# A scheduling model inside the kernel: longer landings for the turned blocks, longer hand-overs between engines, new due times

## The chip, the cores and the metric

The kernel runs on one core of a Trainium2 chip. The metric is the device time of one execution in microseconds (us). Before the change the median of three runs was 1069.37 us (1068.89 to 1074.59).

## The reference

A linear attention with random features, followed by a two-layer network over all tokens:

```python
def phi(x):                       # q and k: (8, 8, 576, 64), scaled
    proj = np.einsum('bhsd,md->bhsm', x, omega)      # 128 features
    h = proj - np.sum(x * x, axis=-1, keepdims=True) / 2.0
    return np.exp(h - np.max(h, axis=-1, keepdims=True)) / np.sqrt(m)
kv = np.einsum('bhsm,bhsd->bhmd', phi(k), v)
z = np.sum(phi(k), axis=2)
attn = np.einsum('bhsm,bhmd->bhsd', phi(q), kv) / (np.einsum('bhsm,bhm->bhs', phi(q), z)[..., None] + 1e-06)
x = attn as (4608 tokens, 512)
h = x @ w_in                      # (512, 2048), float64 weights
out = np.where(h > 0.0, h, np.exp(np.minimum(h, 0.0)) - 1.0) @ w_out
```

## The kernel before

**The network.** 4608 tokens are cut into 12 blocks of 384, and 2048 hidden features into 16 steps f of 128. One step of a block is layer one (tile `ph`, lines 912 to 914: for each of four chunks c three matmuls on 384 columns, high and low halves of operands), the activation (ACT lines 921 and 922, DVE line 925, then `g` in a high and a low half), and layer two (`acc`, lines 950 to 952: for each of three groups of 128 tokens three matmuls on 512 columns). The first three blocks run in two halves of eight steps, while the weights are still being turned from float64 into pairs of float32 (`from_f64`, tile `u_w`; the second layer's halves `w2h`, `w2l` stay on the chip, the first layer's go to DRAM as `w1s` and come back step by step as `w1c`, three buffers). Steps are numbered through all blocks: ph_84, g_85, w1c_89 are steps 84, 85 and 89 of 192.

**The attention.** 64 heads make 32 pairs. Pair i goes through: load of xk, xq and v; projection and exponent for k (`ppk`, line 524, then `hk`); the same for q (`ppq`, `hq`); the state (`pkv`, line 616); the sum of k's features (`zs` on POOL, split into `zr` by ACT and DVE); `pz`, line 673, which spreads that sum; the denominators (`den`, DVE line 694); the normalised `hq` (POOL); then hq is turned so that features lie on partitions (`qh`), and `pn` (line 773) multiplies it with the state. pn goes into `xh` and `xl`, the input of layer one. Four pairs make a batch, 576 tokens, which later blocks of the network read; so attention of later tokens runs between the network's steps of earlier ones.

**The turned pairs.** For pairs 8 to 31 (`TURNED = 8`) hq is turned in three stages: DVE transposes 32 x 32 blocks (`tb`, line 739); one DMA writes them to DRAM (`turned`, line 746, 576 KB); four DMAs fetch them back in the other order (`qh`, line 751, 144 KB each). There is one buffer for qh and four in DRAM.

**What sets the order.** The kernel is written as a list of tasks. `Plan.op` takes a task's engine, its estimated duration, a due time, what it reads and writes, and the bytes of a DMA. `Plan.order` then plays the program through on a model of the chip: at each moment an engine that is free takes, among the tasks whose inputs are ready and whose buffers are free, the one with the earliest due time. The instructions are issued in the order in which the model started them, engine by engine, and each engine then runs its list strictly in that order. When a result counts as ready for the next engine is set by `LAT` (ns, from engine to engine), and a DMA's by `DMA_LAT` (twice, before and after the transfer) and `DMA_RATE`. Some tasks may go to either of two engines (`alt`); the model decides that too. All DMAs are issued by SP, one queue in order. The due times come from numbers at the head of the file: `MLP0`, `SEG`, `STEP`, `STEP_ATT` place the network's steps, `DUE_...`, `LOAD2`, `K2`, `KV2`, `Q2` say how long before its end a pair's parts are due, `EARLIER` brings the loads, projections, pz and denominators of turned pairs forward, and `CONV1` to `CONV3` place the weight conversions.

Of the kernel before, what the change touches and what calls it, by code (L numbers as in the profile page):

```python
# [18 lines left out]
P = 128  # L19
# [12 lines left out]
NJ = 9  # L32
# [8 lines left out]
NNAT = dict(k=7, q=8)  # L41


MLP0 = 44.09
SEG = [8.6, 6.25, 3.85, 5.29, 3.12, 5.81]
STEP = 5.38
STEP_ATT = 6.27

LAG = 3.3


PAIR0 = 9.09
DUE_LOAD, DUE_K, DUE_KV, DUE_Q = 23.0, 24.78, 13.79, 18.96
LOAD2, K2, KV2, Q2 = 69.42, 37.24, 24.66, 31.63
TAIL = 12.51
TAIL2 = 4.95


CONV1 = 12.88
CONV_STEP = -0.22  # L60
CONV2 = 0.04

EARLY = 23.2
CONV3 = 62.36


SPLIT = (0, 8, 16)
NHALF = 3

DUE_Z = 13.27  # L70


TURNED = 8
EARLIER = 6.61
QB = 32
NQB = P // QB
NTURN = 4


NONES = 8  # L80
# [27 lines left out]
class Plan:  # L108
# [2 lines left out]


    LAT = {
        "PE": dict(PE=0, ACT=230, DVE=196, POOL=200, SP=200),
        "ACT": dict(PE=270, ACT=200, DVE=145, POOL=207, SP=200),
        "DVE": dict(PE=250, ACT=128, DVE=127, POOL=203, SP=200),
        "POOL": dict(PE=150, ACT=150, DVE=150, POOL=102, SP=200),
        "SP": dict(PE=100, ACT=100, DVE=100, POOL=100, SP=100),
    }
    LOOSE = ("pa", "h")  # L120

    SHARED = ("DVE", "POOL")

    FREE = dict(PE=1300.0, ACT=1950.0, DVE=2100.0, POOL=1300.0, SP=700.0)
    DMA_LAT, DMA_RATE = 1100.0, 360.0

    def __init__(self):
        self.tasks, self.writer, self.readers = [], {}, {}

    def op(self, eng, ns, due, fn, reads=(), writes=(), nbytes=0, alt=None, port=False, after=0.0):  # L130
        n = len(self.tasks)
        engs = {eng: (ns, 0.0)}
        for e, *t in alt or ():
            engs[e] = tuple(t)
        f = fn if alt is not None else lambda e: fn()
        deps, bufs = set(), set()
        for k in reads:
            if k in self.writer:
                deps.add(self.writer[k])
            self.readers.setdefault(k, []).append(n)  # L140
        for k in writes:
            if k in self.writer:
                deps.add(self.writer[k])
            deps.update(self.readers.pop(k, ()))
            self.writer[k] = n
        for k in (*reads, *writes):
            b = k[0] if isinstance(k, tuple) else k
            if isinstance(b, Buf):
                bufs.add(b)
        deps.discard(n)  # L150
        for b in bufs:
            b.left += 1
        self.tasks.append((engs, due, f, deps, bufs, nbytes, port, after))

    def order(self):
# [7 lines left out]
        end = [0.0] * len(tasks)  # L163
        free, queue, events = {}, {}, [0.0]
        held = dict.fromkeys(self.SHARED, 0.0)
        slots, dma = {}, 0.0
# [47 lines left out]
        while len(done) < len(tasks):  # L214
            started = False
            for eng, q in queue.items():
                if free[eng] > now:
                    continue
                best, first = None, 0.0
                for n in q:  # L220
                    engs, due, _, _, bufs, _, port, _ = tasks[n]
                    if ready[n][eng] > now or (best is not None and due >= first):
                        continue
                    if eng == "DVE" and port and held["POOL"] > now or eng == "POOL" and held["DVE"] > now:
                        continue
                    if len(engs) > 1 and not mine(n, eng):
                        continue
                    for b in bufs:
                        if b.slot is None:
                            s = sum(z <= now for z in slots[b.key])  # L230
                            if s < (1 if line[b.key][-1] is b else 2 if b.key in self.LOOSE else 99):
                                break
                    else:
                        best, first = n, due
                if best is None:
                    continue
                started = True
                engs, _, _, _, bufs, nbytes, port, _ = tasks[best]
                for e in engs:
                    queue[e].remove(best)  # L240
                ns = engs[eng][0]
                for b in bufs:
                    if b.slot is None:
                        s = slots[b.key]
                        b.slot = s.pop(s.index(min(s)))
                        line[b.key].remove(b)
                free[eng] = now + ns
                if eng == "POOL" or eng == "DVE" and port:
                    held[eng] = now + ns
                if nbytes:  # L250
                    dma = max(now + self.DMA_LAT, dma) + nbytes / self.DMA_RATE
                    end[best] = dma + self.DMA_LAT
                else:
                    end[best] = now + ns
                heapq.heappush(events, free[eng])
                done.append((best, eng))
                for b in bufs:
                    b.left -= 1
                    if not b.left:
                        heapq.heappush(events, end[best] + 200.0)  # L260
                        slots[b.key].append(end[best] + 200.0)
                for u in users[best]:
                    for e in ready[u]:
                        ready[u][e] = max(ready[u][e], end[best] + self.LAT[eng][e])
                    waits[u] -= 1
                    if not waits[u]:
                        for e in ready[u]:
                            queue[e].append(u)
                            heapq.heappush(events, ready[u][e])
            if not started:  # L270
                if not events:
                    raise RuntimeError("no task can start")
                now = max(now, heapq.heappop(events))
# [33 lines left out]
def performer_elu_kernel(  # L307
# [14 lines left out]
    nc = tc.nc  # L322
# [35 lines left out]
    op = pl.op  # L358
# [297 lines left out]
    def finish(i, due):  # L656
# [24 lines left out]
        qh = Buf(sb, [P, 2, S], F32, "qh", f"qh_{i}", 1)  # L681
        for g in range(3):
            d = due - 9 + g - early
            js = slice(4 * g, min(4 * g + 4, NJ))
            n = js.stop - js.start
# [38 lines left out]
            def dst(x, g=g):  # L724
# [8 lines left out]
                alt=other("turn", "DVE", dve(n * P)),  # L733
            )
        if i >= TURNED:
            tb = Buf(sb, [P, NQB * NJ * QB], F32, "raw", f"tb_{i}", 4)

            def blocks():
                nc.vector.transpose(
                    out=tb().rearrange("p (n j c) -> p j n c", n=NQB, j=NJ),  # L740
                    in_=h().rearrange("p j (n c) -> p j n c", c=QB),
                )

            op("DVE", 1378, due - 10, blocks, [(h, "n", g) for g in range(3)], (tb,))
            qt = turned[i % NTURN]
            op("SP", 700, due - 9, lambda: nc.sync.dma_start(qt, tb()), (tb,), (("qt", i % NTURN),), P * P * NJ * 4)
            for m in range(NQB):

                def fetch(m=m):
                    r = slice(m * QB, (m + 1) * QB)  # L750
                    nc.sync.dma_start(
                        qh()[r].rearrange("p a (n x) -> p (a n) x", n=2),
                        qt[:, m * NJ * QB:(m + 1) * NJ * QB].rearrange("(n r) x -> r n x", r=QB),
                    )

                op("SP", 600, due - 8 + 0.1 * m, fetch, (("qt", i % NTURN),), ((qh, m),), QB * P * NJ * 4)

        kvf = kvs[i % 2]
        halves = [(slice(o, o + n), n, bank(i, "pa", f"pn_{i}_{o}")) for o, n in ((0, 256), (256, S - 256))]
# [50 lines left out]
    def from_f64(src, hi, lo, nm, due, key):  # L810
# [19 lines left out]
        def ui():  # L830
# [4 lines left out]
            "SP", 500, due - 10, lambda: nc.sync.dma_start(raw(), src), (), ((raw, 0), (raw, 1)), P * 4096,  # L835
            after=due - EARLY,
        )
# [35 lines left out]
    def weights(F, due):  # L873
# [8 lines left out]
        if blk == 0:  # L882
            from_f64(w1[f], lambda: t()[:, 0], lambda: t()[:, 1], f"w1_{f}", due, (t,))
            op("SP", 500, due, lambda: nc.sync.dma_start(w1s[f], flat()), both, (("w1s", f),), P * 4096)
            from_f64(w2[f], lambda: w2h[:, f], lambda: w2l[:, f], f"w2_{f}", due + CONV1 - (CONV2 if f < SPLIT[1] else CONV3), ("w2", f))
        else:
# [89 lines left out]

    begin, t = [], MLP0
    for n, (blk, f0, f1) in enumerate(SEGMENTS):
        begin.append(t)
        t += (f1 - f0) * (SEG[n] if n < len(SEG) else STEP if blk % 3 == 1 or blk >= NBLK - 2 else STEP_ATT)  # L980
    begin.append(t)
# [4 lines left out]
    def batch(b, n):  # L986

        t0, t1 = begin[n - 1], begin[n] - (TAIL if b < 2 else TAIL2)
        for hp in range(NHP):
            pair(b * NHP + hp, t0 + (t1 - t0) * (hp + 1) / NHP)  # L990

    def segment(n):
        blk, f0, f1 = SEGMENTS[n]
        F0 = sum(b - a for _, a, b in SEGMENTS[:n])
        for F in range(F0, F0 + f1 - f0):
            if blk:
                weights(F, step[F])
            layer1(F, step[F])
            layer2(F, step[F] + LAG * STEP)

    def convert(n):
        F0 = sum(b - a for _, a, b in SEGMENTS[:n])
        for e in range(SEGMENTS[n][2] - SEGMENTS[n][1]):
            weights(F0 + e, step[F0 + e] - CONV1 - CONV_STEP * e)

    warm()
    omega(MLP0 - TAIL + PAIR0 * (1 - NHP) - DUE_LOAD)
    for hp in range(NHP):
        pair(hp, MLP0 - TAIL + PAIR0 * (hp + 1 - NHP))
    convert(0)  # L1010
# [91 lines left out]
```

## Time and profile before

| what | before |
|---|---|
| median of three runs | 1069.37 us |
| profiled execution, its own time | 1065.02 us |
| its span | 1063.2 us |
| mean granted TensorE clock | 0.988 |
| moved by DMA | 205.24 MB, mean 193 GB/s |
| L912, L913, L914 (layer one), 768 each | 263.6, 258.6 and 259.1 us busy |
| L950, L951, L952 (layer two), 576 each | 231.3, 228.0 and 228.0 us busy |
| turned<-tb, 24 DMAs, median to landing | 3.2 us |
| qh<-turned, 96 DMAs, to landing, min, median, max | 2.3, 4.3 and 7.8 us |

The profile names engines PE (TensorE), DVE (VectorE), ACT (ScalarE), POOL (GpSimd) and SP. A row of a group gives the line, the engine, the operation, the tiles out<-in without their numbers, the shape, the count; then busy time and mean duration in ns; then how long the engine stood idle just before these instructions, and for what. A row of waits gives engine, tile and line, `<-` what released it, and the total in us, how many times, and the longest. A row of the timeline gives start and duration in us, and in brackets the idle time before it. Matmuls are pipelined: one starts before the last has ended, so the distance of two starts is what a matmul costs.

### The profile page before, as it was taken

The numbers are of one execution on the slowest core, as the hardware profiler recorded it, in microseconds if no ns is written. First come the engines' busy times: TensorE is split into PE (matmuls) and PEld (weight loads), VectorE is DVE, ScalarE is ACT, GpSimd is POOL, SyncE is SP. The second block draws the span as 40 slices with busy tenths as digits, with TensorE's granted clock in tenths as the row PEclk, the third lists the DMA queues.
The fourth block names the chain that finished last, engine by engine and source line by source line (L and its number), as shares of the span: only waits on it lengthen the run. The fifth ranks groups of instructions, "written<-read, shape, count | busy, mean of one in ns | idle before, by whom it ended". The sixth has DMA issues, their size and how long they took to land.

```text
span 1063.2 us, 19120 instructions
## 1 busy us (share of the span) xinstructions
PE 1023.1 (96%) x5923; PEld 899.9 (85%) x5923; DVE 651.1 (61%) x2453; ACT 697.4 (66%) x1887; POOL 414.2 (39%) x419
## 2 busy tenths in 40 slices
PE   8989899999999999999999899999989999999998
PEld 7878788988878788998778788889878888899987
DVE  7989978768877763236757775225777766322221
ACT  7988675569978773358877795327888886332322
POOL 3635433324544443234444454223444444222221
PEclk9989899999999999999999999999999999999999
DMA  8556486567786665435766656534657664443431
GB/s 219 187 186 220 174 280 215 214 228 263 243 294 213 193 209 180 165 114 206 230 202 220 215 201 229 166 132 162 213 181 234 201 204 142 161 159 131 149 131 58
DMA packets 70518, 205.24 MB, mean 193 GB/s; under 512 B 7952, under 2 KB 20432, under 8 KB 70416
## 3 DMA queue, kind: packets, MB, share of 16 engines
q1 hardware_dynamic: 70416, 204.01, 57.8%
q8 instruction: 48, 0.79, 0.3%
q14 instruction: 54, 0.44, 0.1%
HBM read 169.64 MB, written 34.34 MB: 192 GB/s over the span
## 4 chain that ended last, share of the span: by engine, by line
PE 70%; DVE 10%; DMA 8%; ACT 7%; issue 2%; SPq 1%; POOL 0%; DVEq 0%; ACTq 0%; POOLq 0%
PE ph L912 10%; PE acc L950 10%; PE ph L914 10%; PE ph L913 10%; PE acc L951 9%; PE acc L952 9%; DMA qh<-turned 5%; PE pn L773 2%; PE ppq L524 2%; PE ppk L524 2%; PE pkv L575 1%; PE pkv L616 1%; ACT hk L444 1%; DMA xq<-in_qx_dram 1%; ACT hq L444 1%
## 5 line engine op out<-in xcount | busy, mean ns | idle before, releaser
L367 POOL TENSOR_TENSOR g<-e,g 128x384 fp32r<-128x384 f32 x168 | 183.6, 1093 | 419.8 <-DVE g L364 335.4
L912 PE MATMUL ph<-xh,w1c 128*128 128x384 f32 x768 | 263.6, 343 | 0.1
L914 PE MATMUL ph<-xh,w1c 128*128 128x384 f32 x768 | 259.1, 337 | 0.0
L913 PE MATMUL ph<-xl,w1c 128*128 128x384 f32 x768 | 258.6, 337 | 0.0
L921 ACT ACTIVATE e<-ph 128x384 f32<-128x384 f32 x192 | 94.9, 495 | 233.0 <-PE ph L914 230.9
L925 DVE SCALAR_TENSOR_TENSOR e<-e,ph 128x384 f32<-128x384 f32 x192 | 105.7, 551 | 211.3 <-ACT e L922 210.4
L950 PE MATMUL acc<-w2h,g 128*128 128x512 f32 x576 | 231.3, 402 | 0.0
L951 PE MATMUL acc<-w2l,g 128*128 128x512 f32 x576 | 228.0, 396 | 1.6 <-DVE w2l L367 1.6
L952 PE MATMUL acc<-w2h,g 128*128 128x512 f32 x576 | 228.0, 396 | 0.0
L912 PEld LDWEIGHTS ph<-xh,w1c 128*128 128x128 f32 x768 | 145.0, 189 | 15.0 <-issue 2.5
L913 PEld LDWEIGHTS ph<-xl,w1c 128*128 128x128 f32 x768 | 144.9, 189 | 9.7
L914 PEld LDWEIGHTS ph<-xh,w1c 128*128 128x128 f32 x768 | 144.5, 188 | 0.0
L952 PEld LDWEIGHTS acc<-w2h,g 128*128 128x128 f32 x576 | 108.3, 188 | 25.5
L367 POOL TENSOR_TENSOR hq<-hq,den 128x512 f32<-128x512 f32 (+1 forms) x96 | 81.7, 871 | 101.9 <-DVE den L703 77.1
L950 PEld LDWEIGHTS acc<-w2h,g 128*128 128x128 f32 x576 | 108.5, 188 | 13.9 <-issue 2.9
L951 PEld LDWEIGHTS acc<-w2l,g 128*128 128x128 f32 x576 | 108.4, 188 | 11.4 <-DVE w2l L367 1.9
L922 ACT ACTIVATE e<-e 128x384 f32<-128x384 f32 x192 | 101.9, 532 | 3.3
L694 DVE CUSTOM_DVE_ANT_0 junk<-hq,pz 128x128 f32<-128x128 f32 (+1 forms) x320 | 73.6, 278 | 18.9 <-PE pz L673 17.4
L533 ACT ACTIVATE p2k<-ppk,sqk 128x128 f32<-128x128 f32 x225 | 69.9, 370 | 16.2 <-PE ppk L524 13.4
L860 POOL TENSOR_TENSOR u_w<-u_w,raw_w 128x512 int32<-128x512 int32 x32 | 46.6, 1458 | 76.2 <-DVE u_w L857 52.0
L542 DVE CUSTOM_DVE_ANT_0 hq<-ppq,p2q 128x128 f32<-128x128 f32 x216 | 53.2, 286 | 33.4 <-ACT p2q L533 32.2
L444 ACT ACTIVATE hk<-hk,mnk 128x128 f32<-128x128 f32 x225 | 72.0, 408 | 0.1
(101 smaller groups left out, 1539.5 us busy)
## 6 DMA issues: line engine op xcount, KB each, us to landing
w1c<-w1s SPq DMA_DIRECT2D x176, 512.0 KB, 3.3
raw_w<-in_w_dram SPq DMA_DIRECT2D x32, 512.0 KB, 4.5
xk<-in_kx_dram SPq DMA_DIRECT2D x25, 576.0 KB, 4.3
xq<-in_qx_dram SPq DMA_DIRECT2D x24, 576.0 KB, 5.6
turned<-tb SPq DMA_DIRECT2D x24, 576.0 KB, 3.2
qh<-turned SPq DMA_DIRECT2D x96, 144.0 KB, 4.3
v<-in_v_dram SPq DMA_DIRECT2D x32, 325.0 KB, 4.8
out_dram<-o SPq DMA_DIRECT2D x36, 256.0 KB, 3.4
```

The lines of the kernel that those rows point to most:

```text
L367: (nc.vector if e == "DVE" else nc.gpsimd).tensor_tensor(*args)
L444: nc.scalar.activation(h()[:, j, :], src(j), AF.Exp, bias=mn()[:, j:j + 1], scale=-1.0)
L694: nc.vector.tensor_tensor_reduce(out=junk()[r], in0=h()[r, j, :], in1=pz()[r, a * P:(a + 1) * P], scale=1.0, scalar=EPS, op0=ALU.mult, op1 ...
L912: nc.tensor.matmul(ph(), wh, xh[:, c, o:o + TB], start=(c == 0), stop=False)
L913: nc.tensor.matmul(ph(), wh, xl[:, c, o:o + TB], start=False, stop=False)
L914: nc.tensor.matmul(ph(), wl, xh[:, c, o:o + TB], start=False, stop=(c == NC - 1))
L921: op("ACT", act(TB, True), due, lambda: nc.scalar.activation(e(), ph(), AF.Relu, scale=-1.0), (p,), (e,))
L922: op("ACT", act(TB), due + 0.2, lambda: nc.scalar.activation(e(), e(), AF.Exp, scale=-1.0), (e,), (e,))
L925: lambda: nc.vector.scalar_tensor_tensor(e(), e(), -1.0, ph(), ALU.add, ALU.max), (p, e), (e,),
L950: nc.tensor.matmul(a(), g()[:, 0, ts], w2h[:, f], start=(f == f0), stop=False)
L951: nc.tensor.matmul(a(), g()[:, 0, ts], w2l[:, f], start=False, stop=False)
L952: nc.tensor.matmul(a(), g()[:, 1, ts], w2h[:, f], start=False, stop=(f == f1 - 1))
```

## The change

The model gets a new delay, `LAND`: the DMA that stores a turned tile and the four that fetch it count as landing 2000 ns later than by the formula. All entries of `LAT` between different engines grow, by 64 to 300 ns; `DMA_LAT` goes from 1100 to 1500 ns. A turned store or fetch thus counts 2.8 us more than before from issue to use. All due times are set anew; `EARLIER` grows by 4.39 us. No instruction of the program is changed, only the order in which the engines get them, and for tasks with `alt`, which engine. The core of the diff:

```diff
-MLP0 = 44.09
-SEG = [8.6, 6.25, 3.85, 5.29, 3.12, 5.81]
+MLP0 = 45.16
+SEG = [8.6, 5.97, 3.67, 5.16, 3.34, 5.69]
...
-LOAD2, K2, KV2, Q2 = 69.42, 37.24, 24.66, 31.63
+LOAD2, K2, KV2, Q2 = 72.76, 36.27, 29.03, 29.75
...
-CONV1 = 12.88
-CONV_STEP = -0.22
-CONV2 = 0.04
+CONV1 = 11.46
+CONV_STEP = 0.11
+CONV2 = 0.74
...
-CONV3 = 62.36
+CONV3 = 52.47
...
-EARLIER = 6.61
+EARLIER = 11.0
...
+LAND = 2000.0
...
-        "PE": dict(PE=0, ACT=230, DVE=196, POOL=200, SP=200),
-        "ACT": dict(PE=270, ACT=200, DVE=145, POOL=207, SP=200),
-        "DVE": dict(PE=250, ACT=128, DVE=127, POOL=203, SP=200),
-        "POOL": dict(PE=150, ACT=150, DVE=150, POOL=102, SP=200),
-        "SP": dict(PE=100, ACT=100, DVE=100, POOL=100, SP=100),
+        "PE": dict(PE=0, ACT=300, DVE=260, POOL=270, SP=300),
+        "ACT": dict(PE=500, ACT=200, DVE=215, POOL=280, SP=300),
+        "DVE": dict(PE=480, ACT=200, DVE=127, POOL=270, SP=300),
+        "POOL": dict(PE=400, ACT=230, DVE=230, POOL=102, SP=300),
+        "SP": dict(PE=400, ACT=200, DVE=200, POOL=200, SP=200),
...
-    DMA_LAT, DMA_RATE = 1100.0, 360.0
+    DMA_LAT, DMA_RATE = 1500.0, 360.0
...
-                    end[best] = dma + self.DMA_LAT
+                    end[best] = dma + self.DMA_LAT + self.lands[best]
...
-            op("SP", 700, due - 9, lambda: nc.sync.dma_start(qt, tb()), (tb,), (("qt", i % NTURN),), P * P * NJ * 4)
+            op("SP", 700, due - 9, lambda: nc.sync.dma_start(qt, tb()), (tb,), (("qt", i % NTURN),), P * P * NJ * 4, lands=LAND)
...
-                op("SP", 600, due - 8 + 0.1 * m, fetch, (("qt", i % NTURN),), ((qh, m),), QB * P * NJ * 4)
+                op("SP", 600, due - 8 + 0.1 * m, fetch, (("qt", i % NTURN),), ((qh, m),), QB * P * NJ * 4, lands=LAND)
```

What it moves is shown at three places, all of pair 17. In the rows a tile's first number is its pair or step, the last one only tells buffers apart; lines from 113 on are two higher in the changed file.

TensorE around pz_17, before: it stands behind the last part of layer one of step 84 and just ahead of layer two of step 82.

```order
L914 MATMUL ph_84_6123<-xh_88,w1c_84_5924 128x384
L524 MATMUL ppk_18_0_6148<-om_74,tk_18_5939 128x256 x2
L673 MATMUL pz_17_6157<-zr_17_6103,ones_72 128x256 x2
L524 MATMUL ppk_18_1_6160<-om_74,tk_18_5939 128x256 x2
L950 MATMUL acc_5_0_0_6013<-w2h_80,g_82_6088 128x512
```

TensorE around pz_17 in the changed order: it stands behind step 83's layer one, ahead of step 81's layer two and of all projections of pair 18.

```order
L916 MATMUL ph_83_6032<-xh_88,w1c_83_5855 128x384
L627 MATMUL pkv_17_6055<-ident_67,zs_17_5969 128x128
L675 MATMUL pz_17_6101<-zr_17_6071,ones_72 128x256 x2
L952 MATMUL acc_5_0_0_6042<-w2h_80,g_81_6006 128x512
L953 MATMUL acc_5_0_0_6042<-w2l_81,g_81_6006 128x512
```

So pz_17 has moved ahead by about one step of the network.

TensorE ahead of pn_17, before: layer two of step 85 and the first part of step 88's layer one.

```order
L912 MATMUL ph_88_6423<-xh_88,w1c_88_6255 128x384
L913 MATMUL ph_88_6423<-xl_89,w1c_88_6255 128x384
L914 MATMUL ph_88_6423<-xh_88,w1c_88_6255 128x384
L950 MATMUL acc_5_0_2_6050<-w2h_80,g_85_6302 128x512
L951 MATMUL acc_5_0_2_6050<-w2l_81,g_85_6302 128x512
L952 MATMUL acc_5_0_2_6050<-w2h_80,g_85_6302 128x512
L773 MATMUL pn_17_0_6436<-qh_17_6369,kvf1_77 64x256 x2
```

TensorE ahead of pn_17 in the changed order: the same, and one more part of step 88.

```order
L954 MATMUL acc_5_0_2_6074<-w2h_80,g_85_6340 128x512
L914 MATMUL ph_88_6447<-xh_88,w1c_88_6267 128x384
L915 MATMUL ph_88_6447<-xl_89,w1c_88_6267 128x384
L916 MATMUL ph_88_6447<-xh_88,w1c_88_6267 128x384
L775 MATMUL pn_17_0_6475<-qh_17_6326,kvf1_77 64x256 x2
```

So pn_17 has kept its place but for three matmuls, and the stretch between pz_17 and pn_17 has grown from its front.

SP around the store and the fetch of pair 17, before (`turned1` is the DRAM buffer; `xq_20` the load of a later pair's q):

```order
L887 DMA w1c_88_6255<-w1s_82 128x1024
L746 DMA turned1_85<-tb_17_6294 128x1152
L887 DMA w1c_89_6333<-w1s_82 128x1024
L417 DMA xq_20_6351<-in_qx_dram 128x1152
L751 DMA qh_17_6369<-turned1_85 32x4x288 x4
L887 DMA w1c_90_6401<-w1s_82 128x1024
```

SP at the same place in the changed order:

```order
L889 DMA w1c_87_6198<-w1s_82 128x1024
L748 DMA turned1_85<-tb_17_6206 128x1152
L889 DMA w1c_88_6267<-w1s_82 128x1024
L753 DMA qh_17_6326<-turned1_85 32x4x288 x4
L889 DMA w1c_89_6368<-w1s_82 128x1024
L419 DMA v_20_6379<-in_v_dram 128x650
L419 DMA xq_20_6390<-in_qx_dram 128x1152
```

The fetch now stands a step earlier in the stream of w1c loads, and the load of xq_20 has gone from ahead of it to behind it.

More of the change, by code (lines that the diff above doesn't have):

```diff
@@ L41 @@
 NNAT = dict(k=7, q=8)
-MLP0 = 44.09
-SEG = [8.6, 6.25, 3.85, 5.29, 3.12, 5.81]
[L46 to L53, printed above, removed]
-LOAD2, K2, KV2, Q2 = 69.42, 37.24, 24.66, 31.63
-TAIL = 12.51
-TAIL2 = 4.95
-CONV1 = 12.88
-CONV_STEP = -0.22
-CONV2 = 0.04
-EARLY = 23.2
-CONV3 = 62.36
+MLP0 = 45.16
+SEG = [8.6, 5.97, 3.67, 5.16, 3.34, 5.69]
+STEP = 5.29
+STEP_ATT = 6.32
+LAG = 3.35
+PAIR0 = 8.61
+DUE_LOAD, DUE_K, DUE_KV, DUE_Q = 24.84, 25.17, 14.25, 18.96
+LOAD2, K2, KV2, Q2 = 72.76, 36.27, 29.03, 29.75
+TAIL = 12.89
+TAIL2 = 5.01
+CONV1 = 11.46
+CONV_STEP = 0.11
+CONV2 = 0.74
+EARLY = 23.11
+CONV3 = 52.47
 SPLIT = (0, 8, 16)
 NHALF = 3
-DUE_Z = 13.27
+DUE_Z = 13.38
 TURNED = 8
-EARLIER = 6.61
+EARLIER = 11.0
 QB = 32
@@ L124, with op @@
     FREE = dict(PE=1300.0, ACT=1950.0, DVE=2100.0, POOL=1300.0, SP=700.0)
-    DMA_LAT, DMA_RATE = 1100.0, 360.0
+    DMA_LAT, DMA_RATE = 1500.0, 360.0
     def __init__(self):
-        self.tasks, self.writer, self.readers = [], {}, {}
-    def op(self, eng, ns, due, fn, reads=(), writes=(), nbytes=0, alt=None, port=False, after=0.0):
+        self.tasks, self.writer, self.readers, self.lands = [], {}, {}, {}
+    def op(self, eng, ns, due, fn, reads=(), writes=(), nbytes=0, alt=None, port=False, after=0.0, lands=0.0):
         n = len(self.tasks)
+        self.lands[n] = lands
         engs = {eng: (ns, 0.0)}
```

## The prediction

> **What bounds the kernel now.** I read the page's head first, then a table of stretches, then what TensorE waits for, then single places in the timeline.
>
> ```profile
> span 1063.2 us, 19120 instructions
> PE 1023.1 (96%) x5923; PEld 899.9 (85%) x5923; DVE 651.1 (61%) x2453; ACT 697.4 (66%) x1887; POOL 414.2 (39%) x419
> PE 70%; DVE 10%; DMA 8%; ACT 7%; issue 2%; SPq 1%; POOL 0%; DVEq 0%; ACTq 0%; POOLq 0%
> ```
>
> TensorE (PE) is busy for 96% of the span, and the chain of waits runs over it for 70%. The change neither adds nor removes a matmul, so it can win only what lies between matmuls, 40 us in all, and what a lowered clock costs. The table by stretch says where that is (length, then busy time of PE, PEld, DVE, ACT, POOL, then the granted clock):
>
> ```profile
> 0.00:48.00 48.00, 42.40 (x332) 36.62 (x333) 38.63 (x150) 40.20 (x118) 24.53 (x28) 1.00 0.74 212
> 48.00:120.00 72.00, 64.12 (x397) 53.45 (x395) 66.44 (x196) 61.75 (x159) 31.63 (x28) 0.91 0.53 180
> 120.00:165.00 45.00, 44.95 (x229) 39.72 (x229) 37.27 (x96) 28.25 (x61) 19.44 (x14) 0.96 0.73 256
> 165.00:290.00 125.00, 124.40 (x691) 110.95 (x691) 96.87 (x313) 96.64 (x251) 47.24 (x46) 1.00 0.69 233
> 290.00:490.00 200.00, 193.64 (x1127) 170.06 (x1124) 112.53 (x456) 123.01 (x342) 76.66 (x80) 0.99 0.61 199
> 490.00:740.00 250.00, 241.86 (x1415) 213.41 (x1414) 148.53 (x629) 172.52 (x486) 101.54 (x107) 0.99 0.58 193
> 740.00:940.00 200.00, 192.04 (x1151) 168.46 (x1150) 125.66 (x565) 144.16 (x414) 84.85 (x90) 1.00 0.59 193
> 940.00:1063.20 123.20, 119.70 (x596) 107.18 (x595) 25.21 (x56) 30.83 (x60) 28.30 (x28) 1.00 0.34 119
> ```
>
> PE idles 13.5 us up to 165 (5.6, 7.9 and 0.05), 0.6 from 165 to 290, 22.5 from 290 to 940 (6.4, 8.1 and 8.0) and 3.5 in the end, where the last outputs drain. In the long middle part ACT and DVE are busy for about 70% and 60%: they have room. What PE waits for there:
>
> ```profile
> PE pn L773 <- DMA qh<-turned: 16.1, 9, 2.9
> PE ppk L524 <- DVE mnk L542: 2.7, 3, 1.3
> L773 PE MATMUL pn<-qh,kvf 128*64 128x256 f32 x192 | 27.7, 410 | 19.3 <-DMA qh<-turned 16.1 <-DVE tq L367 1.4 <-ACT g L362 1.2
> ```
>
> 19.3 of those 22.5 us stand ahead of one line, L773, the product pn of a turned pair (pairs 8 to 31, eight matmul records each). It reads qh, which has been through DRAM twice. Pair 17 has the longest of these waits. PE first, from the pair's sums pz (L673) to its pn:
>
> ```profile
> 510.57 0.40 PE L673 MATMUL pz<-zr,ones 128*128 128x256 f32 x2
> 510.81 0.40 PE L524 MATMUL ppk<-om,tk 128*128 128x256 f32 x2
> 511.04 0.40 PE L950 MATMUL acc<-w2h,g 128*128 128x512 f32 x1
> 511.28 0.40 PE L951 MATMUL acc<-w2l,g 128*128 128x512 f32 x1
> 512.62 0.34 PE L913 MATMUL ph<-xl,w1c 128*128 128x384 f32 x1
> 512.79 0.34 PE L914 MATMUL ph<-xh,w1c 128*128 128x384 f32 x1
> 530.31 0.40 PE L952 MATMUL acc<-w2h,g 128*128 128x512 f32 x1
> 533.63 1.98 PE L773 MATMUL pn<-qh,kvf 128*64 128x256 f32 x8 [2.92 <-DMA qh<-turned]
> ```
>
> Starts follow each other by 0.23 us on 512 columns, 0.17 on 384, and 0.23 for two on 256; these are the prices below. From the end of pz (510.97) to pn lie 22.7 us, 2.9 of them idle, so PE had 19.7 us of work to put there. Meanwhile the sync engine's queue (SP) did this:
>
> ```profile
> 520.78 0.32 SPq L746 DMA_DIRECT2D turned<-tb  x1
> 522.27 0.32 SPq L887 DMA_DIRECT2D w1c<-w1s  x1
> 523.67 0.33 SPq L417 DMA_DIRECT2D xq<-in_qx_dram  x1
> 524.10 2.11 SPq L751 DMA_DIRECT2D qh<-turned  x4
> ```
>
> The turned tile leaves at 520.8, its fetch is issued from 524.1 to 526.2, and pn can start at 533.6. A load of 576 KB went out just ahead of the fetch.
>
> **The change, part by part.** The edit alters no instruction but the order, and which engine does some copies. **Where pn stands** is the main term. Before, TensorE at pz_17 (ph_84 is a step of layer one, g_82 the one whose layer two follows) and then, 87 rows on, at pn_17: see the order rows ahead of this section. In the changed order pz_17 stands a step of layer one earlier (behind ph_83, with layer two of step 81 next), and pn_17 again behind layer two of step 85, one part of ph_88 later. Counted between pz_17 and pn_17: 36 matmuls on 512 columns before, 45 now; 39 and 54 on 384; 16 and 20 projections on 256; now also one other pair's pn and pz. So the order adds 9 x 0.23 + 15 x 0.17 + 4 x 0.12 = 5.1 us, and with that pn (1.1 by the row of pair 31 below) and pz (0.2) 6.4 us. PE then has 26.1 us of work where the data took 22.7: no wait, with 3.4 us over. Counted the same way, pairs 9 to 31 gain 4.6 us at the least, more than the longest wait, 2.9.
>
> That holds if the data come no later after pz. Pair 31, nearly undisturbed:
>
> ```profile
> 903.48 0.40 PE L673 MATMUL pz<-zr,ones 128*128 128x256 f32 x2
> 914.65 1.74 SPq L751 DMA_DIRECT2D qh<-turned  x4
> 920.02 1.08 PE L773 MATMUL pn<-qh,kvf 128*64 128x256 f32 x8
> ```
>
> Here it is 16.1 us from pz to pn. The 6.6 us that pair 17 takes longer are mostly transfers. In the changed SP order its fetch stands directly behind one w1c load, and xq_20 has moved behind it: the data should come earlier. SP's other moves: the w1c load ahead of a fetch is now one step older, so its slot is free sooner, and the load behind it is needed no earlier than some 27 us after pz, a dozen after the fetch is issued. Where a block ends (pairs 12, 20, 28) the fetch is now split and part of it waits behind the out stores; that is the rival below. I leave **1.5 us** of the 19.3 standing (bounds 0 and 9.6, half), so **-17.8**.
>
> **The clock** after such waits (same columns as the table above):
>
> ```profile
> 368.60:372.10 3.50, 2.25 (x12) 1.71 (x10) 1.81 (x3) 0.84 (x2) 1.68 (x2) 1.00 1.09 187
> 372.10:378.00 5.90, 4.93 (x25) 4.08 (x26) 1.49 (x7) 2.00 (x6) 0.00 (x0) 0.71 0.51 197
> 532.60:540.00 7.40, 6.37 (x34) 5.37 (x35) 2.89 (x22) 2.82 (x9) 0.40 (x1) 0.77 0.45 156
> ```
>
> Behind the waits of pairs 13 and 17 the granted clock was 0.71 over 5.9 us and 0.77 over 7.4: 0.29 x 5.9 and 0.23 x 7.4, 1.7 us each; pn took 1.98 us instead of 1.08 there. Without the waits that goes: **-3.4** (bounds -3.4 and 0).
>
> The Trainium skill ("TensorE: Matmul & The Clock Gate", Part 1 and "Why this matters for your kernels") says that the clock drops to half after a whole idle window of about 3.4 us on a free-running grid. By that rule waits of 2.9 us and less cost nothing more, and the forecast would be 1053. The two rows show the drop after shorter waits, so the rows decide.
>
> **New waits.** pz moves ahead of its old place, and it reads zr, the pair's split sums.
>
> ```profile
> 887.00 0.28 PE L524 MATMUL ppk<-om,tk 128*128 128x256 f32 x1
> 897.21 0.65 DVE L652 TENSOR_TENSOR zr<-zs,zr 128x256 fp32r<-128x256 f32 x1 [0.82 <-ACT zr L649]
> ```
>
> In pair 31 zr was ready 10.6 us after the pair's last ppk. In the changed order the work between the last ppk and pz is 12.4 us at the tightest (pairs 18, 26, 30) and mostly 13 to 16, and zr's steps have earlier due times. Some tight places may wait a little, and the 2.7 us of ppk stay: **+1.5** (bounds 0 and 5).
>
> **The first 165 us.**
>
> ```profile
> 56.27 1.33 PE L768 MATMUL pn<-qh,kvf 128*64 128x320 f32 x4 [2.75 <-ACT hq L444]
> 114.22 0.44 PE L474 MATMUL ppq<-of,xq 128*64 128x128 f32 x4 [1.44 <-ACT hq L444]
> 116.64 0.58 PE L951 MATMUL acc<-w2l,g 128*128 128x512 f32 x1 [1.56 <-DVE w2l L367]
> ```
>
> These waits are on ACT and DVE, which from 48 to 120 are busy for 86% and 92%. This part is bound by how much they do, and the longer hand-overs of the model cannot lessen that. Squares and weight casts move between ACT, DVE and POOL by three or so each, 0.5 to 1.5 us apiece, in both directions. W2's conversion of late steps is due some 3 us sooner, which speaks for the last wait going. I take **0**, bounds -6 and +6: the waits and about half of the 8 us of lost clock (0.09 x 72 + 0.04 x 45) either way. **The end:** the last 642 TensorE rows, from ph_162 on, are in the same order: 0.
>
> Sum against the profiled execution's own 1065.0 us (span 1063.2 and 1.8 around it): -17.8 - 3.4 + 1.5 + 0 = -19.7. The median shown is 1069.4, 4.4 above this execution; applied to it, **1050**.
>
> **The rivals.** *The data come later as well* (it does not do what it says): the fetch is issued later by as much as pn is. For it: the model now lets a fetch wait 2.8 us longer behind the turned store, and other transfers are put between. Against: SP's rows for pair 17, and the 4.6 us. Half the waits and one clock drop stay: -9.6 - 1.7 = -11, 1058. Chance 0.12.
>
> *ACT or DVE becomes the bound.* For it: with 20 us less, both are denser. Against: from 490 to 740 ACT would be busy for 172.5 of 242 us, 71%. In the batches it is higher; half the gain, -10, would be left: 1060. Chance 0.07.
>
> *Slower: the split fetches.*
>
> ```profile
> SPq L972 <- ACT o L362: 50.1, 22, 19.8
> ```
>
> For pairs 12, 20 and 28 SP now holds the rest of a fetch behind the block's last out store, which waits for ACT's copy. Such stores have held the queue 2.3 us on average, and 19.8 once. From that block's last matmul to pn_20 the changed order has 13.5 us of work, and copy, issue and landing (7.3 us for pair 17) need about 11, so a late copy costs from 2.5 us on. To end above 1074.7 (0.5% over 1069.4) the three places must lose 25 us, so each copy must hold the queue 10.8 us, between the mean and the extreme of that row. At 11.5 us each: 3 x 9 = 27 us lost, 1077. Chance 0.05.
>
> **How the numbers follow.** Forecast 0.76 (1041 to 1060), later data 0.12, dense engines 0.07, slower 0.05. The bounds of all terms together give -19.3 - 3.4 + 0 - 6 = -28.7 (1041) and -9.7 + 0 + 5 + 6 = +1.3 (1071). The upper end needs every term at its worst at once, so the range stops where the two rivals with later data and denser engines have most of their weight: 1041 to 1063. A measurement of this kernel can tell about 0.5%, 5.3 us, from no change: faster means under 1064.0. The forecast lies below that; of the two rivals at 1058 and 1060 I put half above it. Faster 0.76 + 0.09 = 0.85, same 0.10, slower 0.05.
>
> **What would show it.** Idle time ahead of L773 (two lines lower in the changed file) falls from 19.3 to under 4 us; PE's idle from 290 to 940 falls from 22.5 to under 8; no clock below 1.00 after 165; pn of pair 17 starts at once. I am wrong if L773 still waits for qh, if pz starts to wait for zr, or if the stretch up to 165 takes over 6 us more.

## The result, and the profile after

| what | before | after |
|---|---|---|
| median, us (runs) | 1069.13, 1065.10 to 1074.59 (4) | 1036.39, 1035.31 to 1038.33 (4) |
| ratio of the times, 95% interval | | 0.9693 [0.9647, 0.9739] |
| profiled execution, its own time | 1065.02 | 1035.31 |
| its span | 1063.2 | 1033.5 |
| mean granted TensorE clock in it | 0.988 | 0.996 |

The changed kernel is 32.7 us faster by the medians and 29.7 us between the two profiled executions. The prediction had 1050 (1041 to 1063), made from a sum of -19.7: the direction was right, the gain was larger than its whole range. Lines from 113 on are two higher in the changed file.

The head of the page after, span, busy time and chain of waits:

```profile
span 1033.5 us, 19113 instructions
PE 1011.9 (98%) x5923; PEld 891.9 (86%) x5923; DVE 669.0 (65%) x2475; ACT 691.5 (67%) x1869; POOL 405.4 (39%) x415
PE 86%; DVE 9%; ACT 2%; DMA 2%; issue 1%; SPq 0%; DVEq 0%; ACTq 0%
```

In the chain DMA has gone from 8% to 2% and ACT from 7% to 2%; DVE kept its 9 to 10%. The table by stretch has the same columns as the one of before (length, busy time of PE, PEld, DVE, ACT, POOL, granted clock, DMA share, GB/s):

```profile
0.00:48.00 48.00, 41.55 (x329) 36.32 (x329) 41.04 (x154) 40.21 (x116) 21.76 (x26) 1.00 0.76 220
48.00:120.00 72.00, 65.21 (x415) 53.17 (x415) 67.57 (x201) 61.57 (x162) 34.68 (x29) 0.95 0.53 178
120.00:165.00 45.00, 42.09 (x219) 36.45 (x218) 39.30 (x86) 26.30 (x58) 18.59 (x16) 1.00 0.73 264
165.00:290.00 125.00, 124.41 (x711) 111.03 (x710) 106.29 (x344) 98.98 (x261) 55.22 (x53) 1.00 0.69 235
290.00:490.00 200.00, 199.17 (x1154) 176.88 (x1155) 120.32 (x492) 131.12 (x365) 77.27 (x83) 1.00 0.63 206
490.00:740.00 250.00, 249.97 (x1483) 220.84 (x1482) 158.48 (x652) 178.71 (x500) 98.40 (x105) 1.00 0.63 206
740.00:940.00 200.00, 199.92 (x1176) 176.50 (x1175) 117.35 (x512) 130.96 (x367) 78.19 (x85) 1.00 0.57 185
```

From 165 to 940 PE is idle for 0.59 + 0.83 + 0.03 + 0.08 = 1.5 us, where it was 23.1, and the clock stands at 1.00 throughout. Up to 165 it is idle for 16.1 us instead of 13.5, at a better clock (0.95 and 1.00 for 0.91 and 0.96); that is now most of its idle time. What PE still waits for from 290 to 940, with pn's group row:

```profile
PE ppq L526 <- DVE mnq L544: 0.5, 1, 0.5
PE pkv L618 <- DVE xl L795: 0.3, 1, 0.3
L775 PE MATMUL pn<-qh,kvf 128*64 128x256 f32 x192 | 26.0, 392 | 0.0
```

The 19.3 us ahead of pn are gone, and so are the 2.7 us ahead of ppk. Pair 17 again, TensorE and SP from pz to pn:

```profile
494.97 0.48 PE L675 MATMUL pz<-zr,ones 128*128 128x256 f32 x2
503.21 0.32 SPq L748 DMA_DIRECT2D turned<-tb  x1
506.85 1.86 SPq L753 DMA_DIRECT2D qh<-turned  x4
520.75 1.08 PE L775 MATMUL pn<-qh,kvf 128*64 128x256 f32 x8
```

The four fetches by themselves, the view of tile qh (duration of an issue in ns, first and last start, then time to landing):

```profile
L753 SPq DMA_DIRECT2D qh<-turned x4: 423/428/438, 506.9 to 508.3; - x4
...
DMA to landing us min/median/max: 3.9/4.2/4.3
```

From pz's end (495.45) to pn are 25.3 us, all of them work (26.1 were counted from the order). The last fetch was issued at 508.3 and landed by 512.6. The data now come 17.2 us after pz instead of 22.7, and lie ready for 8 us. Here pn was moved away from its data, and the data came earlier as well: 2 of the 5.5 us lie ahead of the store (7.8 us after pz instead of 9.8), and some 3 in the landing (3.9 to 4.3 us, where it was 6.7 to 7.8 and a load of 576 KB had gone out just ahead of the fetch; that this load is the cause was not tested).

Pair 17 is not the rule. Pair 31, whose rows of before stand in the prediction, in the changed kernel:

```profile
870.52 0.40 PE L675 MATMUL pz<-zr,ones 128*128 128x256 f32 x2
885.27 1.74 SPq L753 DMA_DIRECT2D qh<-turned  x4
893.72 1.08 PE L775 MATMUL pn<-qh,kvf 128*64 128x256 f32 x8
```

The fetch starts 14.3 us after the end of pz, where it was 10.8, and pn 22.8, where it was 16.1. Worked out in the same way from the starts and landings in the two traces, the data of pairs 9 to 31 land 20.6 us after pz in the median, 17.1 before, and later than before in 18 of the 23 pairs; pn stands at 23.8, 17.5 before. So in most pairs the data come later after pz, and pn has moved away by nearly twice as much. Pair 22 has the least to spare, 0.2 us.

**At equal work.** The third line of layer two has 576 rows, three for each step, so the start of its 123rd row marks step 40 and that of its last row step 191. Up to the first of these every kernel below has started the same matmuls but for three (1688 to 1691 of 5923). Step 40 stands at 295.8 before and at 294.3 after; the last row closes the ranges here (first and last start), before and after:

```profile
L952 PE MATMUL acc<-w2h,g x576: 388/394/632, 71.6 to 1059.3; 128*128 128x512 f32 x192
L954 PE MATMUL acc<-w2h,g x576: 388/389/421, 72.4 to 1029.2; 128*128 128x512 f32 x192
```

So the first 295 us give 1.5 us, and the stretch from step 40 to step 191 gives 28.6.

### The profile page after: what moved, and what is told of

Read it like the earlier page. It is cut to its first block, busy times and chain, and to the rows that moved or that the text cites. A ratio compares the mean times of both kernels' runs of the same rounds, so it can differ in the third digit from the quotient of the medians.

```text
span 1033.5 us, 19113 instructions
## 1 busy us (share of the span) xinstructions
PE 1011.9 (98%) x5923; PEld 891.9 (86%) x5923; DVE 669.0 (65%) x2475; ACT 691.5 (67%) x1869; POOL 405.4 (39%) x415
## 4 chain that ended last, share of the span: by engine, by line
PE 86%; DVE 9%; ACT 2%; DMA 2%; issue 1%; SPq 0%; DVEq 0%; ACTq 0%
PE ph L914 12%; PE acc L952 12%; PE ph L916 12%; PE ph L915 12%; PE acc L953 12%; PE acc L954 12%; PE pkv L618 3%; PE ppk L526 3%; PE ppq L526 2%; PE pn L775 2%; DVE u_w L850 1%; DVE junk L696 1%; DVE u_w L859 1%; PE pkv L577 1%; PE ppq L476 1%
## 5 line engine op out<-in xcount | busy, mean ns | idle before, releaser
L369 POOL TENSOR_TENSOR g<-e,g 128x384 fp32r<-128x384 f32 x173 | 189.5, 1096 | 411.9 <-DVE g L366 343.7
L544 DVE CUSTOM_DVE_ANT_0 hq<-ppq,p2q 128x128 f32<-128x128 f32 x216 | 53.5, 287 | 26.4 <-ACT p2q L535 25.3
```

Source lines behind the costliest of these rows:

```text
L369: (nc.vector if e == "DVE" else nc.gpsimd).tensor_tensor(*args)
```

## The experiments

All in one table; each is told below. "Idle" is PE's, from the table by stretch of the profiled execution; "step 40" and "step 191" are that execution's starts as above, from the start of its span, as differences from before. Each is one execution: the order of before with pn freed is the same order up to step 40, and still comes 1.4 us later there. The ratio is to the kernel before, run on the same chip.

| kernel | median (range), us | ratio [95%] | idle to 165 | idle 165 to 940 | step 40 | step 191 |
|---|---|---|---|---|---|---|
| before | | | 13.5 | 23.1 | 0 | 0 |
| changed kernel | 1036.39 (1035.31 to 1038.33) | 0.9693 [0.9647, 0.9739] | 16.1 | 1.5 | -1.5 | -30.1 |
| order of before, pn freed | 1051.66 (1049.55 to 1056.44) | 0.9829 [0.9762, 0.9896] | 12.7 | 7.9 | +1.4 | -12.2 |
| DMA delays alone | 1045.27 (1044.80 to 1047.86) | 0.9770 [0.9719, 0.9820] | 19.8 | 4.2 | +7.1 | -17.2 |
| hand-overs alone | 1064.33 (1058.53 to 1068.24) | 0.9927 [0.9895, 0.9958] | 17.3 | 22.5 | +5.6 | +0.8 |
| due times alone | 1048.48 (1047.44 to 1048.93) | 0.9793 [0.9744, 0.9843] | 18.8 | 5.5 | +6.1 | -16.8 |
| changed, old hand-overs | 1046.83 (1046.43 to 1047.65) | 0.9797 [0.9766, 0.9828] | 18.8 | 5.6 | +9.5 | -17.9 |
| changed, old DMA delays | 1045.75 (1044.11 to 1049.48) | 0.9791 [0.9755, 0.9827] | 21.9 | 4.5 | +6.8 | -19.5 |
| changed, old `EARLIER` | 1044.40 (1042.64 to 1045.63) | 0.9772 [0.9740, 0.9805] | 15.3 | 8.9 | -0.3 | -19.4 |
| new model, old due times | 1053.83 (1051.25 to 1057.31) | 0.9865 [0.9821, 0.9910] | 21.1 | 7.4 | +9.2 | -11.9 |
| changed, pn freed | 1035.22 (1034.95 to 1036.19) | 0.9653 [0.9622, 0.9684] | 16.1 | 1.3 | -1.5 | -30.1 |
| hand-overs alone, pn freed | 1043.75 (1042.18 to 1046.37) | 0.9726 [0.9688, 0.9764] | 16.6 | 3.3 | +5.9 | -19.0 |

**1. What the wait for qh is worth, with nothing moved.** The order of every engine is that of before; pn of the turned pairs reads w2h, which is long there:

```diff
-                    q = qh().rearrange("p a (n j c) -> p (a n) j c", n=2, j=NJ)
+                    q = w2h.bitcast(F32).rearrange("p f m -> p (f m)")[:, 0:2 * S].rearrange("p (a n j c) -> p (a n) j c", a=2, n=2, j=NJ)
```

> The kernel before in its own order on every engine; only pn of the turned pairs (8 to 31) reads a tile that lies on the chip all the time, so the product is of other numbers and pn no longer waits for the fetch. Theory A (the gain is PE's wait at pn, with the clock that drops after it): the idle time ahead of pn goes from 19.3 us to under 3, no lowered clock after 165 us, time 1069 - 19 - 3 = 1047 (1040 to 1052), and 10 to 14 us of the change's 33 are left to other causes. Rival B (the waits only move: PE then waits as long at ppk, pz or layer one): over 1060. Rival C (all of the change's gain is these waits): 1036 to 1039.

Measured: 1051.66 us, near the upper end of theory A's range. The ratio is worth 18 us (0.0171 x 1072), and between steps 40 and 191 of the profiled execution 13.6 us are gone, not the 19.3 of idle time and 3.4 of clock. The group rows of pn and ppk from 290 to 940, of before and then of this kernel, show where the rest is:

```profile
L773 PE MATMUL pn<-qh,kvf 128*64 128x256 f32 x190 | 27.4, 409 | 19.3 <-DMA qh<-turned 16.1 <-DVE tq L367 1.4 <-ACT g L362 1.2
L524 PE MATMUL ppk<-om,tk 128*128 128x256 f32 x180 | 36.6, 286 | 2.7 <-DVE mnk L542 2.7
...
L773 PE MATMUL pn<-w2h,kvf 128*64 128x256 f32 x192 | 25.9, 391 | 0.0
L524 PE MATMUL ppk<-om,tk 128*128 128x256 f32 x180 | 38.0, 291 | 6.9 <-DVE mnk L542 3.4 <-DVE den L703 2.9 <-ACT kvf L362 0.4
```

The wait ahead of ppk grows from 2.7 to 6.9 us: the pauses at pn had given DVE time to finish what the projections need. The clock doesn't recover either, as this kernel's rows by stretch show (0.99 in the first and the last):

```profile
290.00:490.00 200.00, 197.65 (x1146) 173.06 (x1145) 116.41 (x482) 125.75 (x349) 78.17 (x81) 0.99 0.62 201
490.00:740.00 250.00, 248.18 (x1453) 218.06 (x1452) 152.96 (x650) 177.26 (x503) 103.72 (x109) 1.00 0.62 199
740.00:940.00 200.00, 196.81 (x1162) 172.01 (x1161) 120.96 (x529) 139.37 (x400) 84.32 (x89) 0.99 0.62 193
```

The lowered clock now stands behind waits ahead of ppk (1.26 and 0.46 us up to 378.2, 1.82 us up to 783.9):

```profile
378.20:381.60 3.40, 3.39 (x11) 3.31 (x12) 2.97 (x13) 2.84 (x10) 2.81 (x3) 0.51 0.00 0
784.40:787.80 3.40, 3.40 (x11) 3.21 (x12) 2.61 (x9) 2.89 (x11) 3.00 (x4) 0.51 0.01 2
```

So the order of before has a second limit right behind the first.

**2. The parts of the change, one at a time.** Three kernels, each the kernel before with one part: `LAND` with `DMA_LAT`; the table `LAT`; all due times with `EARLIER`.

```diff
+LAND = 2000.0
-    DMA_LAT, DMA_RATE = 1100.0, 360.0
+    DMA_LAT, DMA_RATE = 1500.0, 360.0
```

> The kernel before with LAND = 2000 and DMA_LAT = 1500, old hand-overs and old due times. Theory A: pn is put later, PE's idle time ahead of it falls under 5 us, time about 1048 (1042 to 1056). Rival D (the due times are needed, since pn's own delay pushes xh and xl against the next block): waits of layer one for xl at the blocks' starts, time over 1060. Rival E (hand-overs or due times bring the gain): 1065 or more.

```diff
-        "ACT": dict(PE=270, ACT=200, DVE=145, POOL=207, SP=200),
-        "DVE": dict(PE=250, ACT=128, DVE=127, POOL=203, SP=200),
+        "ACT": dict(PE=500, ACT=200, DVE=215, POOL=280, SP=300),
+        "DVE": dict(PE=480, ACT=200, DVE=127, POOL=270, SP=300),
...
```

> The kernel before with the longer hand-overs (LAT) alone. Theory A: pn's wait stays (15 us or more idle ahead of it), small waits at ppk and pz go, time 1060 to 1066. Rival E: under 1055.

```diff
-LOAD2, K2, KV2, Q2 = 69.42, 37.24, 24.66, 31.63
+LOAD2, K2, KV2, Q2 = 72.76, 36.27, 29.03, 29.75
...
-EARLIER = 6.61
+EARLIER = 11.0
...
```

> The kernel before with all due times and EARLIER of the change, but the model's old delays (LAT, DMA_LAT, no LAND). Theory A: pn is put where the model thinks the data are there, as before, so its wait stays (over 12 us idle), time 1058 to 1070. Rival F (starting pz and the denominators 4.4 us sooner is what makes the data early): idle under 6 us, time 1045 to 1052.

pn's group row in each, in this order (DMA delays, hand-overs, due times):

```profile
L775 PE MATMUL pn<-qh,kvf 128*64 128x256 f32 x192 | 26.0, 392 | 0.0
L775 PE MATMUL pn<-qh,kvf 128*64 128x256 f32 x192 | 26.0, 390 | 19.6 <-DMA qh<-turned 15.6 <-DVE tq L369 1.9 <-DVE tk L369 1.1
L775 PE MATMUL pn<-qh,kvf 128*64 128x256 f32 x192 | 26.0, 391 | 1.3 <-DVE mnk L544 0.7 <-PE pkv L627 0.3 <-DMA qh<-turned 0.2
```

The DMA delays alone take the wait away, as the theory had it. The hand-overs alone leave it as it was. The due times alone take it away too, and that was the miss here: the theory was that without the longer delays in the model the fetch and pn keep their distance and the wait stays. With the new due times, pz and the denominators among them, the data also come before pn.

Each part alone also costs 5.6 to 7.1 us up to step 40, which the full change does not. The losses are not at one line. The largest waits of PE from 10 to 200 us with the DMA delays alone were these, with its row by stretch from 48 to 120:

```profile
PE ppk L526 <- DVE mnk L544: 3.2, 3, 1.8
PE ppq L476 <- ACT hk L446: 2.6, 2, 2.0
PE pt L719 <- DVE xl L795: 1.6, 1, 1.6
...
48.00:120.00 72.00, 60.73 (x387) 48.74 (x385) 69.02 (x198) 57.14 (x154) 30.32 (x27) 0.98 0.59 194
```

They are on DVE and ACT, which are busy there for 69.0 and 57.1 of 72 us.

**3. The changed kernel with one part taken back.** Three kernels, and a fourth that has the whole model with all old due times.

```diff
-        "ACT": dict(PE=500, ACT=200, DVE=215, POOL=280, SP=300),
+        "ACT": dict(PE=270, ACT=200, DVE=145, POOL=207, SP=200),
...
```

> The changed kernel with the old hand-overs (LAT). Theory G (the due times are set for the whole model: with any part of it taken back, the first 165 us get slower, as in the runs of single parts, and the middle stays nearly free of waits): idle time of PE up to 165 us 18 to 20 instead of 16, from 165 to 940 under 5, time 1041 to 1047. Rival H (the longer hand-overs take away the projections' waits, lines 524 of before): idle from 165 to 940 over 6, with ppk and ppq in front, 1042 to 1050. Rival I (hand-overs are worth nothing here): 1035 to 1039.

```diff
-LAND = 2000.0
+LAND = 0.0
...
-    DMA_LAT, DMA_RATE = 1500.0, 360.0
+    DMA_LAT, DMA_RATE = 1100.0, 360.0
```

> The changed kernel without LAND and with DMA_LAT = 1100. Theory G: no wait at pn even so, since the earlier due times do that alone; slower only in the first 165 us, 1040 to 1047. Rival J (LAND is needed once the hand-overs are long): over 5 us idle ahead of pn, 1045 to 1055. Rival I (worth nothing here): 1035 to 1039.

```diff
-EARLIER = 11.0
+EARLIER = 6.61
```

> The changed kernel with EARLIER = 6.61 again, so projections, pz and denominators of the turned pairs are due 4.4 us later. Theory G: the model's DMA delays still keep pn behind the fetch, idle ahead of pn under 3 us, time 1037 to 1046. Rival F (EARLIER is what makes the data early): over 6 us idle ahead of pn, 1045 to 1058.

```diff
-LOAD2, K2, KV2, Q2 = 72.76, 36.27, 29.03, 29.75
+LOAD2, K2, KV2, Q2 = 69.42, 37.24, 24.66, 31.63
...
-EARLIER = 11.0
+EARLIER = 6.61
...
```

> The kernel before with the whole new model (LAT, DMA_LAT, LAND), old due times. Theory G: middle part free of waits at pn, first 165 us slower than before by 4 to 8 us, time 1042 to 1048. Rival K (the model alone brings all of it): 1035 to 1039.

Taking back any one part costs 8 to 10 us (ratios of 0.9772 to 0.9797, where the changed kernel has 0.9693), and two kinds of loss can be told apart. Without the hand-overs, or without the DMA delays, the middle stays nearly as good (27.4 and 26.4 us from step 40 to 191, where the full change has 28.6), and the loss comes in the first 295 us (+9.5 and +6.8); theory G nearly held: without the hand-overs the idle time from 165 to 940 is 5.6 us where it had under 5, and without the DMA delays pn waits for 1.4 us where it had none. With the old `EARLIER` it is the other way round: nothing is lost early (-0.3), and the middle gives 19.1 us. pn does not wait there either; what PE waits for from 165 to 940 is

```profile
PE ph L914 <- DVE e L927: 4.6, 6, 1.4
PE ppk L526 <- DVE den L705: 1.7, 1, 1.7
PE ppk L526 <- DVE xl L795: 1.2, 1, 1.2
```

So `EARLIER` isn't needed for qh once the DMA delays are in the model; it takes away short waits for DVE. The new model with the old due times is slower (1053.83) than theory G had it (1042 to 1048), and slower than the DMA delays alone (1045.27). So where the DMA delays are in the model, the longer hand-overs gain 10 us with the new due times and cost 9 with the old ones. Up to step 40 the kernels with nothing lost are those in which model and due times belong together: both old (before, 0), or both new (the change, -1.5; with the old `EARLIER`, -0.3). All six mixtures lose 5.6 to 9.5 us.

**4. Is anything left at pn, and what do the hand-overs do?** The edit of the first experiment, made in the changed kernel and in the kernel with the hand-overs alone (pn's output has other numbers in both).

> The changed kernel, its order on every engine unchanged, but the product pn of the turned pairs reads w2h, which is long there, in place of qh; its output has other numbers there. Theory: in the changed order nothing is left to win at pn, since its data are early: the same time as the changed kernel, 1036 us, from 1034 to 1039; PE idle 1 to 2 us from 165 to 940, 15 to 17 up to 165. Rival: part of pn's waits is left but hidden in other rows or in a lower clock: 1028 to 1033.

> The longer hand-overs alone in the model, and pn of the turned pairs reads w2h in place of qh; its output has other numbers there. With the hand-overs alone TensorE stood idle 22.5 us from 165 to 940, 19.6 of it ahead of pn; in the order of before, with pn freed in the same way, 7.9 us were left, since the waits partly moved to the projections. Theory H: the longer hand-overs are what places the projections so that they don't wait even when pn doesn't hold TensorE back: middle idle under 4, time 1043 to 1047. Rival: the hand-overs do nothing for that, the waits move on as in the order of before: middle idle 6 to 10, time 1048 to 1054.

In the changed kernel it makes no difference (1035.22 and 1036.39, with ranges that overlap): the wait for qh is used up. With the hand-overs alone it takes 1064.33 to 1043.75, and theory H held, with 3.3 us of idle time in the middle. The rows of ppk from 290 to 940, with the hand-overs alone, then with pn freed too, then of the changed kernel, and behind the dots with the DMA delays alone and of the changed kernel with the old hand-overs:

```profile
L526 PE MATMUL ppk<-om,tk 128*128 128x256 f32 x180 | 37.1, 286 | 0.0
L526 PE MATMUL ppk<-om,tk 128*128 128x256 f32 x180 | 37.7, 287 | 1.1 <-DVE den L696 0.6 <-DVE mnk L544 0.4
L526 PE MATMUL ppk<-om,tk 128*128 128x256 f32 x180 | 35.7, 289 | 0.1
...
L526 PE MATMUL ppk<-om,tk 128*128 128x256 f32 x180 | 35.5, 287 | 0.3 <-DVE den L696 0.2
L526 PE MATMUL ppk<-om,tk 128*128 128x256 f32 x180 | 34.8, 287 | 0.5 <-DVE den L696 0.5
```

Freeing pn in the order of before brought ppk to 6.9 us of waiting; with the hand-overs in the model it is 1.1. They are not the only way, though: the last two rows have the old hand-overs, pn doesn't wait there either, and ppk waits for 0.3 and 0.5 us. From step 40 to 191 the kernel before gains 13.6 us by the freeing alone, 4.8 us by the hand-overs alone (+5.6 to +0.8), and 24.9 us by both: more than half of what the hand-overs can give there is hidden as long as pn waits.

## Why the prediction was right in direction and too small

**Where pn stands, -17.8; the clock, -3.4: right, though the condition failed.** More work between pz and pn took the waits away, as foretold. The idle time ahead of pn is 0.0 (1.5 us was left standing, under 4 was forecast), the clock is 1.00 from 165 to 940, and pn's own mean fell from 410 to 392 ns. Idle time gone (19.3) and clock (3.4) make 22.7, against 21.2 in the sum. "That holds if the data come no later after pz" was not met: in the median they land 3.5 us later (20.6 for 17.1). It did no harm, since pn moved by 6.3. The DMA delays alone, and the due times alone, show that this result had two independent causes; the prediction spoke only of the order that came out.

**The new waits, "+1.5 (bounds 0 and 5)", "the 2.7 us of ppk stay": the step that failed.** It was given no gain side. It took the longer hand-overs as something that moves pz and might make a few places tight. The runs show the opposite sign: pz doesn't wait for zr anywhere, and ppk's wait went from 2.7 to 0.1 us. No one part of the change is needed for that: ppk waits for 0.0 us with the hand-overs alone, 0.3 with the DMA delays alone, 1.1 with the due times alone and 0.5 in the changed kernel with the old hand-overs. By subtraction the term is -28.6 + 22.7 = -5.9 from step 40 to 191 where +1.5 stood. That is 7.4 of the 10.4 us between the sum and step 191; 1.5 us left standing at pn and 1.5 us up to step 40 are the rest. Of the 5.9 us, 2.6 are ppk's idle time. The other 3 us or so are in no row of idle time. About half of them are hidden in the waits themselves, since matmuls that follow each other overlap, and those that wait don't. An example from before:

```profile
304.86 0.34 PE L914 MATMUL ph<-xh,w1c 128*128 128x384 f32 x1
306.17 0.48 PE L524 MATMUL ppk<-om,tk 128*128 128x256 f32 x2 [0.97 <-DVE mnk L542]
```

The two starts are 1.31 us apart instead of 0.17, so the wait cost 1.14 us where its row counts 0.97. Over the 22 waits of before from step 40 to 191, less the 4 of the changed kernel, this comes to 1.6 us, an estimate from the starts in the two traces. What is left of the 3 us no run separated.

The same step hid a danger on the other side. Where only pn was mended, in the order of before, 13.6 us of the 22.7 came: 4.2 us of the wait moved on to ppk, and the clock stayed at 0.99 in two stretches, now behind waits at ppk. The sum of idle times ahead of one line was too much for a mend at that line alone, and too little for a change that also moves the line behind it.

**The first 165 us, 0 (bounds -6 and +6): right, but by cancelling.** Idle time grew by 2.6 us, and the clock gave back about 0.04 x 72 + 0.04 x 45 = 4.7 us; step 40 comes 1.5 us sooner, about what two executions of one order differ by there (1.4). The bounds were too narrow for what such edits do there: mixtures of the same parts cost 5.6 to 9.5 us. Which moves cost them isn't settled; the waits are many, 1 to 4 us each, on DVE and ACT.

**The median.** The sum was made against the profiled execution, 1065.0, and laid on the median, 4.4 us above it. Between the profiled executions it is 10.0 us short (-19.7 for -29.7), on the medians 13.6 (1050 for 1036.39): after the change the median lies only 1.1 us above the profiled execution, so most of those 4.4 us went too. Where they come from is told in the last section.

**The rivals.** *Later data*: half of it came. Pair 17's come 5.5 us earlier after pz, but those of 18 of the 23 pairs later, by 3.5 us in the median; pn was moved by more, and none waits. *Dense engines*: no, ACT and DVE are busy for 178.71 and 158.48 of 250 us from 490 to 740 and PE waits for neither. *Split fetches*: they are split, over 5 us for pair 20, but its pn (the first of the last row, pairs 20 and 21) starts at 589.9, 6.5 us after the last issue has ended, and doesn't wait:

```profile
578.38 0.38 SPq L753 DMA_DIRECT2D qh<-turned  x1
579.11 0.34 SPq L974 DMA_DIRECT2D out_dram<-o  x1
580.18 0.95 SPq L974 DMA_DIRECT2D out_dram<-o  x2
581.18 2.23 SPq L753 DMA_DIRECT2D qh<-turned  x3
...
L775 PE MATMUL pn<-qh,kvf x16: 379/379/430, 589.9 to 609.8; 128*64 128x256 f32 x16
```

## What to carry to other kernels

Where a planner's delays are corrected, the wait that they describe is only the first part of the gain: ask which short waits stand right behind it, and give such a term bounds on both sides of nothing. To see what one wait is worth, free it with the order unchanged (let its reader read something that is long there); in this kernel that gave 13.6 of 22.7 us and showed the next limit. Due times that were tuned to one model belong to it: six mixtures of this change's parts lost 5.6 to 9.5 us up to step 40, and all of it together nothing. And look at several of the items that a wait is about, not only at the one with the longest wait: here that one's data came earlier and most others' later.

## What the runs showed of the hardware that was not expected

The time of the kernel before scatters with its clock, and that of the kernel after doesn't. In 13 runs on one chip the kernel before took 1064.03 us at a mean granted clock of 0.992 and 1078.15 at 0.978: 0.014 of the time is 15 us, and the difference is 14.1. The order isn't strict: two of the runs at 0.988 are 5.2 us apart. The four runs of the changed kernel lie at 0.996 to 0.998, within 3.0 us. The kernels whose pn still waits for qh (before, hand-overs alone) spread over 7.9 to 14.1 us in seven to thirteen runs on one chip; those without that wait over 1.2 to 6.9 us, though in four runs each. The widest of these, 6.9 us at 0.988 to 0.992, is the order of before with pn freed, where waits at ppk have taken the place of the wait for qh.

The likely reason is that a wait of TensorE now and then brings a stretch of lowered clock behind it. The prediction's rows show this behind the waits of pairs 13 and 17, and the first experiment's rows at half clock behind waits of 1.3 and 0.5 us close together and of 1.8 us. It isn't so behind every wait. The waits of pairs 13 and 25, in the same execution of the kernel before:

```profile
373.07 1.97 PE L773 MATMUL pn<-qh,kvf 128*64 128x256 f32 x8 [2.23 <-DMA qh<-turned]
787.70 1.08 PE L773 MATMUL pn<-qh,kvf 128*64 128x256 f32 x8 [2.71 <-DMA qh<-turned]
```

Pair 25 waits longer, and yet its pn takes the usual 1.08 us; the granted clock from 787.7 to 793 is 1.00. What decides between them is open; no run tested it by itself.
